# A sum on VectorE replaced by a casting and an adding transfer of GpSimd, in three pairs of row blocks

## The chip, the cores and the metric

The kernel runs on one core of a Trainium2 chip. The metric is the device time of one execution, in microseconds (us). Executions of the kernel before the change took 200.71 us (median of 3, 200.53 to 200.73). The engines are TensorE (PE; PEld is its weight load), VectorE (DVE), ScalarE (ACT), GpSimd (POOL) and SyncE (SP), which here only issues transfers.

## The reference, cut to what matters

The reference normalises x, and adds to x a linear attention of 32 heads and a gated feed-forward block:

```
xn = _layernorm(x, axis=-1)                       # x is 2048 x 512
return x + _A_ref(xn, A_wqkv, A_wo) + _B_ref(xn, B_w_gate, B_w_up, B_w_down)
# _B_ref: (silu(x @ w_gate) * (x @ w_up)) @ w_down, inner width 1792
# _A_ref: q, k, v = x @ wqkv; o = phi(q) (phi(k)^T v) / (phi(q) . sum phi(k)); o @ wo
```

The change lies in the last product, h @ w_down, where h = silu(x @ w_gate) * (x @ w_up) is 2048 x 1792.

## The kernel before, in words

The kernel lists every operation of every engine in one order written out by hand. A small recorder (`_Program`) gives each operation the semaphore waits that its reads and writes need, and each engine then takes its own operations strictly in that order. So an operation that waits holds up all that stands behind it on its engine. A transfer has a semaphore of its own, and whoever reads its result waits for that; the engine that issues it goes on.

Until about 154 us the kernel normalises and transposes x, makes q, k and the attention's matrix M, and makes h in transposed form (14 chunks of 128 columns). Rows 0 to 511 are finished on the way. The last stage, from about 154 us on, makes the output of rows 512 to 2047: six **pairs** p = 0 to 5 of row blocks, 128 rows each, `PAIRS = (10, 4, 12, 14, 6, 8)`, block `PAIRS[p]` and the next. A pair's h (256 rows x 1792) times w_down (1792 x 512) is a 2 x 2 block product, done with seven products in the place of eight (Strassen's way, in Winograd's form). It needs four sums of the quarters A11, A12, A21, A22 of h, each 128 x 896:

- `hcopy(p, i)` (L1055, ACT): scales one of four pieces of h into the pair's own buffers, in bf16. Piece 0 (7 chunks) holds A11 and A21, in buffer `Lo[p % 2]`; pieces 1, 2, 3 (2, 3 and 2 chunks) hold A12 and A22, in `Hi[p % 3]`. The tiles' names in the trace are those of the memory reused: `Lo` is wqkv or GT; `Hi` is xn, ef or xnT; piece 0 reads hT, piece 3 reads pq.
- `h_sum(p, i)` (L1067, DVE), in f16: S0 = A21 + A22, S1 = S0 - A11, S2 = A11 - A21, S3 = A12 - S1. The four lie in `Sd[p % 2]`.
- `dprod(p, i, ...)` (L1083, PE): product i, seven matmuls of 128x256. Products 5, 6, 7, 3 read S0, S1, S2, S3; products 1, 2, 4 read A11, A12, A22. `first(p)` is product 1 and the copy `dseed` (L1095, ACT); it is done in the pair before.
- `attn` (L1089, PE): four matmuls that add the attention of one block and one half of the columns; they read pk, which is q divided and transposed.
- `dkeep` (L1099, ACT), `dkeep_y` (L1103, DVE) and `du4` (L1109, DVE) carry partial results between banks of PSUM; `dout` (L1115, DVE) makes a 128 x 256 piece of output, and `store` (L692, SP) sends it.

Beside these runs the division of q for one block per pair, for use in later pairs: `den_sum` (L644, DVE), `den_turn` (L650, DVE, writes rden), `pq_mul` (L654, POOL, waits for rden), `turn` (L660, SP, a transposing transfer pk<-pq), and `pz_ahead` (L638, POOL, pz for the block two places on). There are two buffers of pz; the one made in pair p is read by the `den_sum` of pair p + 2, or by the second `den_sum` of pair 4.

In the order of pair p from 2 to 4, DVE takes S3 of p, den_sum, den_turn, dkeep_y, du4, one output, S0 of p + 1, one output, S1 of p + 1, one output, S2 of p + 1, one output. PE takes products 5 and 2 of p, two groups of attn, product 6, product 1 of p + 1, products 7 and 3, attn, product 4, attn. Which copies stand where on ACT is a table `HC`: key (pair, place), where place 0 is after dkeep, place 1 after dkeep_y, place 2 after `first(p + 1)`.

Nothing is issued as a transfer from GpSimd in the kernel before.

Of the kernel before, what the change touches and what calls it, by code (L numbers as in the profile page):

```python
# [7 lines left out]
ALU = mybir.AluOpType  # L8
# [109 lines left out]
def bass_parallel_sum__linear_attn_block__swiglu_ffn__prompt_kernel(nc, A_x, A_wqkv, A_wo, B_x, B_w_gate, B_w_up, B_w_down, out):  # L118
    xin = A_x[0]
    oview = out[0]  # L120
    K = _Program()
    bf, f32 = dt.bfloat16, dt.float32

    with contextlib.ExitStack() as es:
# [91 lines left out]
        def B(i):  # L216
            return ("bank", i)
# [424 lines left out]
        def den_sum(t):  # L642
            i = SLOT[t] % 2
            K.add("dve", lambda e: e.tensor_reduce(  # L644
                out=den[:, i, :], in_=pzh[i], axis=mybir.AxisListType.X, op=ALU.add),
                r=[("pz", i)], w=[("den", i)])

        def den_turn(t):
            i = SLOT[t] % 2
            K.add("dve", lambda e: e.reciprocal(rden[:, i, :], den[:, i, :]), r=[("den", i)], w=[("rden", i)])  # L650

        def pq_mul(t, after=()):
            i = SLOT[t] % 2
            K.add("pool", lambda e: e.tensor_tensor(  # L654
                out=heads(pq[:, t, :]), in0=heads(pq[:, t, :]),
                in1=rden[:, i, :][:, :, None].broadcast_to([P, NH, DH]), op=ALU.mult),
                r=[("pq", t), ("rden", i)] + list(after), w=[("pq", t)])

        def turn(t):
            K.add("sp", lambda e: e.dma_start_transpose(  # L660
                out=pk[:, SLOT[t], :].rearrange("p (g s) -> p g s", g=NG), in_=pq[:, t, :]),
                r=[("pq", t)], w=[("pk", SLOT[t])], dma=True)
# [323 lines left out]
        def split(ap):  # L986
            return ap.rearrange("p (s c) -> p s c", s=2)
# [13 lines left out]
        def wt(n):  # L1001
            return [("Wt", n, 0), ("Wt", n, 1)]

        def k7(ap):
            return ap.rearrange("p (k c) -> p k c", k=7)
# [9 lines left out]
        def t_sum(i, h):  # L1015
            own = {2: wtk, 3: [("xs", 0), ("xs", 1)], 4: late}[i]
            a, b, rk = {2: (Wt[2], Tt[1], [("Wt", 22, h)] + tk(1, h)), 3: (Tt[2], Wt[1], tk(2, h) + [("Wt", 11, h)]),
                        4: (Wt[3], Tt[2], [("Wt", 21, h)] + tk(2, h))}[i]
            K.add("dve", lambda e: e.tensor_tensor(
                out=Tt[i][:, h, :], in0=a[:, h, :], in1=b[:, h, :], op=ALU.subtract), r=rk, w=[("Tt", i, h)], a=own)  # L1020

        def tk(i, h=None):
            ks = [("Tt", i, g) for g in ((0, 1) if h is None else (h,))]
            return [k_ + (c,) for k_ in ks for c in (0, 1)] if i == 1 else ks
# [10 lines left out]
        def Av(p, i):  # L1035
            return (Lo[p % 2] if i % 2 == 0 else Hi[p % 3])[:, :, (i // 2) * P:(i // 2 + 1) * P]

        def Ak(p, j):
            return ("Lo", p % 2) if j == 0 else ("Hi", p % 3, j)
        Sd = [[xnf[:, 10 * D + 2 * N7:10 * D + 3 * N7], xnT[:, 0, 0:N7], pqf[:, 10 * D:10 * D + N7], xnT[:, 0, N7:2 * N7]],  # L1040
              [xnT[:, 1 + i // 2, (i % 2) * N7:(i % 2 + 1) * N7] for i in range(4)]]
        Sd = [[k7(s_.bitcast(f16)) for s_ in r] for r in Sd]
# [16 lines left out]
        H0, H1 = (0,), (1, 2, 3)  # L1059

        def h_sum(p, i):
            r = p % 2
            A11, A12, A21, A22 = [Av(p, j) for j in range(4)]
            S_ = Sd[r]
            a, b, op, hs, more = ((A21, A22, ALU.add, H0 + H1, []), (S_[0], A11, ALU.subtract, H0, [0]),
                                  (A11, A21, ALU.subtract, H0, []), (A12, S_[1], ALU.subtract, H1, [1]))[i]
            K.add("dve", lambda e: e.tensor_tensor(out=S_[i], in0=a, in1=b, op=op),  # L1067
                  r=[Ak(p, j) for j in hs] + [("Sd", r, j) for j in more], w=[("Sd", r, i)], a=sdk[r][i] if p < 2 else ())

        def dk(b):  # L1070
            return banks[b][:, 0:HD]

        def dprod(p, i, b, start, ks=range(7)):
            r = p % 2
            n = {5: 1, 6: 2, 7: 3, 4: 4, 1: 11, 2: 21, 3: 22}[i]
            cut, rk = (Tt[n], tk(n)) if n < 10 else (Wt[BS[n]], wt(n))
            if i in (1, 2, 4):
                L = Av(p, {1: 0, 2: 1, 4: 3}[i])
                lk = [Ak(p, j) for j in (H0 if i == 1 else H1) if any(0 <= k + 7 * (i > 1) - PIECE[j][0] < PIECE[j][1] for k in ks)]
            else:  # L1080
                j = {5: 0, 6: 1, 7: 2, 3: 3}[i]
                L, lk = Sd[r][j], [("Sd", r, j)]
            K.add("pe", [(lambda e, k=k: e.matmul(  # L1083
                split(banks[b][:, 0:HD]), L[:, k, :], cut[:, :, k * P:(k + 1) * P], start=(start and k == 0), stop=False,
                skip_group_check=True)) for k in ks], r=lk + rk, w=[B(b)])

        def attn(p, s_, lo, b):
            t = PAIRS[p] + s_
            K.add("pe", [(lambda e, g=g: e.matmul(dk(b), pk[:, SLOT[t], g * P:(g + 1) * P], M[:, g, lo:lo + HD], start=False,  # L1089
                                                  stop=(g == NG - 1), skip_group_check=True)) for g in range(NG)],  # L1090
                  r=[("pk", SLOT[t])] + [("M", g) for g in range(NG)], w=[B(b)])
# [5 lines left out]
        def dkeep(p):  # L1097
            r, d = p % 2, GB[p % 2][2]
            K.add("act", lambda e: e.activation(p5[:, r, 0:HD], dk(d), ACT.Copy), r=[B(d)], w=[("p5", r)])  # L1099
# [20 lines left out]
        def pz_ahead(t, after=()):  # L1120
            i = SLOT[t] + 2
            if i < NT:
                pz_mul(ORDER[i], after)
# [8 lines left out]
        for fc in range(NFC):  # L1132
# [13 lines left out]
            p = fc // 2  # L1146
# [65 lines left out]
        def first(p):  # L1212
            a, b, d = GB[p % 2]
            dprod(p, 1, a, True)
            dseed(p)

        DIV2 = {1: 15, 2: 6, 3: 7, 4: 9, 5: 8}
        HC = {(0, 1): [(1, 1), (1, 2), (1, 3)], (0, 2): [(2, 1), (2, 2), (2, 3)], (1, 0): [(2, 0)], (1, 1): [(3, 1)]}
        HC.update({(p, 2): [(p + 2, 0), (p + 2, 2)] for p in (1, 2, 3)})
        HC.update({(p, 0): [(p + 1, 3)] for p in (2, 3, 4)})  # L1220
        HC.update({(p, 1): [(p + 2, 1)] for p in (2, 3)})

        def copies(p, i):
            for v in HC.get((p, i), ()):
                hcopy(*v)
# [5 lines left out]
        for p in range(NP2 - 1):  # L1231
            a, b, d = GB[p % 2]
            t = DIV2.get(p)
            if p == 0:
                attn(p, 0, 0, a)
            dprod(p, 5, d, True)
            dkeep(p)
            if p == 0:
                t_sum(3, 0)
                t_sum(3, 1)  # L1240
                h_sum(0, 2)
            else:
                copies(p, 0)
                if p > 1:
                    h_sum(p, 3)
                den_sum(t)
                den_turn(t)
                pq_mul(t)
                turn(t)
            dprod(p, 2, a, False)  # L1250
            if p:
                attn(p, 0, 0, a)
            attn(p, 1, HD, d)
            dkeep_y(p)
            copies(p, 1)
            dprod(p, 6, b, False)
            if p == 0:
                first(1)
            du4(p, d)
            if p:  # L1260
                dout(p, 0, 0, a)
            if p == NP2 - 2:
                den_sum(DIV2[p + 1])
            if p == 0:
                h_sum(0, 3)
                t_sum(4, 0)
                t_sum(4, 1)
                copies(p, 2)
            else:
                if p == 1:  # L1270
                    h_sum(1, 3)
                h_sum(p + 1, 0)
                first(p + 1)
                copies(p, 2)
            dprod(p, 7, b, False)
            dout(p, 1, HD, b)
            if p == 0:
                dout(0, 0, 0, a)
                h_sum(1, 0)
            h_sum(p + 1, 1)  # L1280
            if p == NP2 - 2:
                den_turn(DIV2[p + 1])
            elif p:
                pz_ahead(t, [("Sd", 0, 0)] if p == 1 else [])
            dprod(p, 3, d, False)
            attn(p, 0, HD, d)
            dout(p, 0, HD, d)
            h_sum(p + 1, 2)
            if p == NP2 - 2:
                pq_mul(DIV2[p + 1], [("Sd", (p + 1) % 2, 2)])  # L1290
                turn(DIV2[p + 1])
            dprod(p, 4, b, False)
            attn(p, 1, 0, b)
            dout(p, 1, 0, b)
        p = NP2 - 1
# [58 lines left out]
```

## Time and profile before

| | |
|---|---|
| median of 3 runs | 200.71 us |
| the profiled execution | 200.89 us, its span 199.6 us |
| PE busy in the span | 195.1 us (98%) |
| DVE, ACT, POOL busy | 170.5, 153.6, 122.3 us |
| from the start of pair 2 to the end of pair 4 (169.69 to 190.97 us) | PE busy 7.09 of 7.09, 7.10 of 7.10, 7.09 of 7.09 us |
| the same, DVE busy | 6.78, 6.19, 6.22 us |
| the same, POOL busy | 2.17, 2.18, 1.06 us |

The profile is of one execution. Times in it count from the start of its span. The 1.3 us between span and time lie outside what it shows. A row of the timeline is: start, length, engine, line, operation, tile written <- tiles read, shapes, and in brackets how long the engine had been idle and what ended that.

### The profile page before, as it was taken

To read this page: it belongs to the slowest core of one execution; us is meant where nothing else is said; L and a number is where in the kernel's file an instruction comes from. 1 tells how busy PE (TensorE), PEld (TensorE's weight loads), DVE (VectorE), ACT (ScalarE), POOL (GpSimd) and SP (SyncE) were. 2 spreads that over 40 slices of the span, in tenths; PEclk is the share of its full clock that TensorE was granted. 3 is DMA by queue.
4 is the path that set the end of the run, shared out by engine and by line. 5 is a ranking of instruction groups with operands and counts; after the bars stand their busy time and mean duration, and the time that the engine had idled before them with its cause. 6 is when DMAs were issued, how large, how long until landed. Compare 5 with 4: busy or idle time off the path is not lost.

```text
span 199.6 us, 3566 instructions
## 1 busy us (share of the span) xinstructions
PE 195.1 (98%) x1193; PEld 114.8 (58%) x1207; DVE 170.5 (85%) x339; ACT 153.6 (77%) x308; POOL 122.3 (61%) x150
## 2 busy tenths in 40 slices
PE   8899999999999999999999999999999999999995
PEld 2344444444544445555555555555555888888884
DVE  2999998894797798988888998887799999998866
ACT  3799887749889988689898988888989968475200
POOL 3687876799995544787677666768877004413220
DMA  6943243289990000011111221000210012132223
GB/s 180 355 122 81 57 87 73 50 282 364 375 295 3 0 3 0 0 28 31 26 26 26 53 56 23 4 0 7 45 34 0 3 39 66 30 79 66 45 69 118
DMA packets 28899, 15.97 MB, mean 80 GB/s; under 512 B 17232, under 2 KB 28880, under 8 KB 28880
## 3 DMA queue, kind: packets, MB, share of 16 engines
q1 hardware_dynamic: 28320, 15.28, 27.3%
q10 hardware_dynamic: 560, 0.46, 0.7%
q8 instruction: 9, 0.15, 0.3%
q14 instruction: 10, 0.08, 0.1%
HBM read 9.70 MB, written 2.10 MB: 59 GB/s over the span
## 4 chain that ended last, share of the span: by engine, by line
PE 94%; DVE 2%; DMA 2%; issue 1%; ACT 0%; POOL 0%; SPq 0%
PE pb L846 32%; PE pb L1083 16%; PE pb L431 13%; PE pb L556 12%; PE pb L480 7%; PE pb L682 6%; PE pb L1089 5%; PE pb L686 2%; DMA x_sb<-in_A_x_dram 2%; PE pb L605 1%; PE pb L674 0%; DVE pq L470 0%; PE pb L398 0%; POOL ef L459 0%; DVE stats L298 0%
## 5 line engine op out<-in xcount | busy, mean ns | idle before, releaser
L654 POOL TENSOR_TENSOR pq<-pq,rden 128x512 bf16<-128x512 bf16 x16 | 16.9, 1056 | 36.7 <-DVE rden L650 23.1
L868 ACT ACTIVATE zacc<-pb,iw 128x384 bf16<-128x384 f32 x56 | 31.3, 590 | 5.9 <-PE pb L846 4.7
L431 PE MATMUL pb<-wqkv,xnT 128*128 128x512 bf16 x110 | 25.1, 379 | 0.2
L846 PE MATMUL pb<-xnT,wg 128*128 128x384 bf16 x112 | 25.1, 326 | 0.0
L638 POOL TENSOR_TENSOR pz<-pq,zbc 128x512 f32<-128x512 bf16 x16 | 18.6, 1164 | 5.3 <-DVE ef L808 3.8
L883 POOL TENSOR_TENSOR hT<-c,zacc 128x384 bf16<-128x384 f32 x18 | 16.1, 915 | 6.0 <-DVE c L879 4.0
L459 POOL TENSOR_SCALAR ef<-ef 128x512 bf16<-128x512 bf16 x25 | 15.5, 620 | 5.8 <-ACT ef L452 5.6
L879 DVE TENSOR_TENSOR c<-pb,p 128x384 f32<-128x384 f32 x28 | 15.5, 555 | 4.1 <-PE pb L846 2.8
L431 PEld LDWEIGHTS pb<-wqkv,xnT 128*128 128x128 bf16 x112 | 10.9, 98 | 13.3 <-DVE pk L470 0.4
L452 ACT ACTIVATE ef<-pb 128x512 bf16<-128x512 f32 x25 | 14.8, 593 | 3.9 <-PE pb L431 3.9
L874 DVE TENSOR_TENSOR pb<-pb,p 128x384 f32<-128x384 f32 x28 | 15.3, 561 | 1.7 <-PE pb L846 0.9
L497 POOL TENSOR_TENSOR zacc<-zacc,pk 128x512 f32<-128x512 f32 x13 | 15.4, 1181 | 1.0
L856 ACT ACTIVATE pb<-pb 128x384 f32<-128x384 f32 x28 | 12.7, 473 | 3.8 <-PE pb L846 2.9
L846 PEld LDWEIGHTS pb<-xnT,wg 128*128 128x128 bf16 x112 | 10.6, 98 | 7.7 <-ACT pb L856 0.8
L556 PE MATMUL pb<-xnT,wg 128*128 128x512 bf16 x56 | 14.7, 379 | 0.0
L556 PE MATMUL pb<-xnT,wu 128*128 128x512 bf16 x53 | 14.3, 379 | 0.1
L846 PE MATMUL pb<-xnT,wqkv 128*128 128x384 bf16 x56 | 13.7, 326 | 0.0
L846 PE MATMUL pb<-GT,wqkv 128*128 128x384 f16 x56 | 13.7, 326 | 0.0
L846 PE MATMUL pb<-wo,wqkv 128*128 128x384 f16 x56 | 13.7, 326 | 0.0
L298 DVE BATCH_NORM_STATS2 stats<-x_sb 128x6 f32<-128x512 bf16 x16 | 10.8, 678 | 3.0 <-DMA x_sb<-in_A_x_dram 3.0
L1089 PE MATMUL pb<-M,pk 128*128 128x256 bf16 x96 | 13.4, 273 | 0.0
L480 PE MATMUL pb<-pk,xn 128*128 128x512 bf16 x55 | 12.5, 379 | 0.1
(210 smaller groups left out, 488.6 us busy)
## 6 DMA issues: line engine op xcount, KB each, us to landing
x_sb<-in_A_x_dram SPq DMA_DIRECT2D x14, 128.0 KB, 4.5
wg<-in_B_w_gate_dram SPq DMA_DIRECT2D x2, 896.0 KB, 8.3
wu<-in_B_w_up_dram SPq DMA_DIRECT2D x2, 896.0 KB, 9.6
wd<-in_B_w_down_dram SPq DMA_DIRECT2D x2, 896.0 KB, 13.7
out_dram<-out_sb SPq DMA_DIRECT2D x24, 64.0 KB, 1.6
wqkv<-in_A_wqkv_dram SPq DMA_DIRECT2D x3, 256.0 KB, 5.0
wqkv<-in_A_wqkv_dram SPq DMA_DIRECT2D x1, 512.0 KB, 9.0
wo<-in_A_wo_dram SPq DMA_DIRECT2D x1, 512.0 KB, 10.0
```

Of the source, the lines that this page charges most:

```text
L431: K.add("pe", [(lambda e, c=c: e.matmul(banks[b][:, :], src[:, c, t * P:(t + 1) * P], wqkv[:, c, col:col + D], start=(c == 0), stop=(c == ...
L459: K.add("pool", lambda e: e.tensor_scalar(out=buf, in0=buf, scalar1=top, scalar2=0.0, op0=ALU.min, op1=ALU.max), r=[bkey] + tkeys, w=[bkey])
L480: K.add("pe", [(lambda e, c=c: e.matmul(banks[c][:, :], src[:, t, c * P:(c + 1) * P], pk[:, t, :], start=first, stop=last)) for c in range ...
L556: fns.append(lambda e, c=c, b=b, w_=w_: e.matmul(banks[b][:, :], w_[:, c, fc * P:(fc + 1) * P], xnT[:, c, C * 512:(C + 1) * 512], start=(c ...
L638: K.add("pool", lambda e: e.tensor_tensor(out=pzh[i][:, :, 0:DH], in0=heads(pq[:, t, :]), in1=heads(zbc[:, :]), op=ALU.mult), r=[("pq", t) ...
L654: K.add("pool", lambda e: e.tensor_tensor(out=heads(pq[:, t, :]), in0=heads(pq[:, t, :]), in1=rden[:, i, :][:, :, None].broadcast_to([P, N ...
L846: K.add("pe", [(lambda e, c=c: e.matmul(banks[bank][:, 0:TS], L[i][:, c, :], R[i][:, c, ts], start=(start and c == 0), stop=(c == 1), skip ...
L868: K.add("act", lambda e: e.activation(sil4[:, n, :], bk(bank), ACT.Silu, scale=iw[:, 0:1]), r=[B(bank), ("iw",)], w=[("sil4", n), ("zacc", ...
L879: K.add("dve", lambda e: e.tensor_tensor(out=c22[:, q, :], in0=bk(b), in1=p5[:, q, :], op=ALU.add), r=[B(b), ("p5", q)], w=[("c22", q)])
L883: K.add("pool", lambda e: e.tensor_tensor(out=hj(fc)[:, TB + q * TS:TB + (q + 1) * TS], in0=c22[:, q, :], in1=sil4[:, 2 * q + 1, :], op=AL ...
L1083: K.add("pe", [(lambda e, k=k: e.matmul(split(banks[b][:, 0:HD]), L[:, k, :], cut[:, :, k * P:(k + 1) * P], start=(start and k == 0), stop ...
L1089: K.add("pe", [(lambda e, g=g: e.matmul(dk(b), pk[:, SLOT[t], g * P:(g + 1) * P], M[:, g, lo:lo + HD], start=False, stop=(g == NG - 1), sk ...
```

## The change

The sums S0 of pairs 3, 4 and 5 are no longer made by DVE. In each of the pairs p = 2, 3, 4 GpSimd issues two transfers from one part of the core's memory to another: `h_acc(p + 1, 0)` copies A21 into S0's place, casting from bf16 to f16, and `h_acc(p + 1, 1)` adds A22 to it. The first stands ahead of pq_mul on POOL, the second behind it and ahead of pz_ahead. The second waits for the first to have landed. Both are 128 x 7 x 128 elements; the source lies in rows of 128 elements (256 bytes) with gaps, the destination is without gaps. S0 of pairs 0, 1 and 2 stays on DVE.

To have A22 complete sooner, piece 3 of pair p + 2 is copied by ACT at place 1 of pair p, behind piece 1, and no longer at place 0 of pair p + 1. This holds for pairs 3, 4 and 5.

```diff
+        def h_acc(p, i):
+            S_, src = Sd[p % 2][0], Av(p, 2 + i)
+            how = {} if i == 0 else dict(accum_op=ALU.add)
+            K.add("pool", lambda e: e.dma_start(S_, src, **how),
+                  r=[Ak(p, j) for j in (H1 if i else H0)] + ([("Sd", p % 2, 0)] if i else []), w=[("Sd", p % 2, 0)], dma=True)
...
-        HC.update({(p, 0): [(p + 1, 3)] for p in (2, 3, 4)})
-        HC.update({(p, 1): [(p + 2, 1)] for p in (2, 3)})
+        HC.update({(p, 1): HC.get((p, 1), []) + [(p + 2, 3)] for p in (1,)})
+        HC.update({(p, 1): [(p + 2, 1), (p + 2, 3)] for p in (2, 3)})
...
                 copies(p, 0)
                 if p > 1:
+                    h_acc(p + 1, 0)
+                if p > 1:
                     h_sum(p, 3)
                 den_sum(t)
                 den_turn(t)
                 pq_mul(t)
                 turn(t)
+                if p > 1:
+                    h_acc(p + 1, 1)
...
                 if p == 1:
                     h_sum(1, 3)
-                h_sum(p + 1, 0)
+                if p == 1:
+                    h_sum(2, 0)
                 first(p + 1)
                 copies(p, 2)
```

## The prediction

> **What bounds the kernel.** I read the chain that ended last first, then busy time by stretch for pairs 2 to 4, then the timeline of each engine there, then the transfers.
>
> ```profile
> PE 94%; DVE 2%; DMA 2%; issue 1%; ACT 0%; POOL 0%; SPq 0%
> ```
> ```profile
> 169.69:176.78 7.09, 7.09 (x67) 6.29 (x65) 6.78 (x14) 4.49 (x6) 2.17 (x2) 1.00 0.22 58
> 176.78:183.88 7.10, 7.10 (x68) 6.34 (x66) 6.19 (x13) 4.49 (x6) 2.18 (x2) 1.00 0.22 55
> 183.88:190.97 7.09, 7.09 (x67) 6.34 (x65) 6.22 (x15) 1.36 (x3) 1.06 (x1) 1.00 0.24 59
> ```
>
> The columns of the second fence are the stretch, its length, and busy PE, PEld, DVE, ACT, POOL, then clock, DMA share, GB/s. The stretches run from product 5 of a pair to product 5 of the next. PE has no gap: 65 matmuls at 0.109 us (0.765 us for seven, 172.09 to 172.85) are 7.09 us. The clock is full. DVE has 0.3 to 0.9 us spare in each. So work taken off DVE here shortens nothing; what can happen is that PE begins to wait.
>
> ```profile
> 169.69 0.93 PE L1083 MATMUL pb<-mixb,xn 128*128 128x256 f16 x7
> ...
> 176.78 0.93 PE L1083 MATMUL pb<-mixb,xnT 128*128 128x256 f16 x7
> ...
> 172.00 0.35 DVE L650 RECIPROCAL rden<-den 128x32 f32<-128x32 f32 x1
> ...
> 173.79 1.30 DVE L1067 TENSOR_TENSOR xnT<-GT,xn 128x896 f16<-128x896 bf16 x1
> 175.01 0.47 DVE L1115 SCALAR_TENSOR_TENSOR out_sb<-pb,iso,c 128x256 bf16<-128x256 f32 x1
> 175.40 0.61 DVE L1067 TENSOR_TENSOR xnT<-xnT,GT 128x896 f16<-128x896 f16 x1
> ...
> 178.66 0.35 DVE L650 RECIPROCAL rden<-den 128x32 f32<-128x32 f32 x1
> ...
> 167.83 1.17 POOL L638 TENSOR_TENSOR pz<-pq,zbc 128x512 f32<-128x512 bf16 x1 [1.56 <-DVE xn L1067]
> 172.43 1.05 POOL L654 TENSOR_TENSOR pq<-pq,rden 128x512 bf16<-128x512 bf16 x1 [3.43 <-DVE rden L650]
> 173.44 1.16 POOL L638 TENSOR_TENSOR pz<-pq,zbc 128x512 f32<-128x512 bf16 x1
> ```
>
> These are product 5 of pairs 2 and 3; DVE's rden of pair 2, S0 of pair 3 (the 1.30 row, slowed beside POOL; elsewhere 0.61), an output, S1 of pair 3, rden of pair 3; and POOL. See where the adding transfer must fit: behind pq_mul of pair 2 (ends 173.48), ahead of S1 (175.40) and product 5 (176.78).
>
> ```profile
> DMA packets 6470, 2.57 MB, mean 51 GB/s; under 512 B 3136, under 2 KB 6464, under 8 KB 6464
> ...
> q1 hardware_dynamic: 6464, 2.49, 18.8%
> ...
> out_dram<-out_sb SPq DMA_DIRECT2D x24, 64.0 KB, 1.6
> ...
> pk<-pq SPq DMA_TRANSPOSE x5, 2.4
> ```
>
> These are the transfers from 150 us on. A packet takes 0.188 x 49.6 x 16 / 6464 = 23 ns of one of 16 engines. The five transposing transfers are all there is under 512 bytes: 627 packets each, 2.4 us from issue to landing, of which SP issues for 1.2 us. A store of 128 packets lands in 1.6 us.
>
> **The change, part by part.**
>
> *S0 off DVE.* Three instructions (1.30, 0.87 and 0.61 us; 0.4 to 0.6 us of queue each) go. Worth 0: PE has no gap to close.
>
> *Piece 3 sooner on ACT.* In pair 1 one copy (0.71 us) comes ahead of dseed of pair 2. ACT was idle 0.50 us there, so dseed (166.63) and the two copies behind it move by 0.2 us; ACT's next idle time, 1.14 us before 170.65, takes that up, and dseed's bank is read by product 6 only at 172.09. In pairs 2 and 3 two short copies stand behind dkeep as before, only other ones. Cost 0, covered by those idle times. The buffers overwritten were last read by product 4 of a pair earlier (168.49 for the copy into ef, which now comes after 171).
>
> *The copying transfer.* POOL issues it after pz_mul (169.0) and piece 0 (168.9 with the shift). The adding one comes at 173.48, so it has 4.5 us to land at no cost. POOL itself is idle until 172.43; 3.4 us of issuing are free. If POOL issued longer, pq_mul would wait, and behind it turn on SP, whose pk is read two pairs on (180.18 plus 2.4 against attn of pair 4 at 185.41): cover enough.
>
> *The adding transfer* stands ahead of pz_mul on POOL. That pz is read by den_sum two pairs on (185.01) or in pair 4 (187.98), so up to 3 us of issue cost nothing. What waits for it is DVE (S1), then PE (product 5, which reads S0).
>
> Call its time from issue to landing X. No transfer is issued by GpSimd in this trace, so X is bounded. From below: the store, 1.6 us. Nearest row: the transposing transfer, inside the core's memory and in pieces of 256 bytes; this one has 128 x 7 = 896 pieces. Scaled: issue 1.2 x 896 / 627 = 1.7, pieces 896 x 23 ns / 16 = 1.3, and the rest of the 2.4 (2.4 - 1.2 - 0.9 = 0.3): 3.3 us for the copying one. The adding one reads its destination too; that is 0 to 1.3 us more, I take half: X = 4.0. From above: issue and pieces twice as dear, 2 x 3.0 + 0.3 = 6.3. I take 4.0, nearest to the row with the most alike pieces.
>
> Now the loop. S1 waits for the landing T. Behind it on DVE stand an output, S2, an output, S3, den_sum and rden: spacings 0.53 + 0.40 + 0.53 + 0.40 + 0.54 + 0.74 + 0.35 = 3.49 us (175.40 on, waits taken out). Then pq_mul, 0.08 + 1.05, and only then POOL issues the next pair's adding transfer. So T(next) = T + 3.49 + 1.13 + X, while PE needs T every 7.09 us.
> - Pair 3: T = 173.5 + 4.0 = 177.5; product 5 was at 176.78: PE waits 0.72.
> - Pair 4: T = 177.5 + 4.62 + 4.0 = 186.1; PE would be at 183.88 + 0.72: 1.5 more.
> - Pair 5: T = 194.7 against 190.97 + 2.2: 1.5 more.
> - In pair 5 the division of the last block hangs behind S1 and S2 as well: S2 ends T + 1.7, pq_mul T + 2.85, turn lands 2.4 later, T + 5.3; the attn that reads it stands at T + 5.03 (196.00 - 190.97). 0.3 more.
> - du4 of the pair comes T + 4.4, product 3 at T + 4.69: no wait.
>
> Sum 0 + 0 + 0.7 + 1.5 + 1.5 + 0.3 = 4.0 to 4.1 us, in general 3X - 8.2 + 0.3 once X is over 2.7. On the profiled execution 200.89 + 4.1 = 205.0; it is 0.2 above the median of the runs, so against that 200.7 + 4.1 = 204.8 us.
>
> The Trainium skill (DMA: Bandwidth & Descriptors, Anatomy of one DMA — SWDGE (gpsimd) path) gives a GpSimd transfer about 2.0 us and its bytes at 436 GB/s; by it 229 KB would take an estimated 2.5 us and the sum would be 0. No run here shows it yet.
>
> **Rivals.**
> - *The transfer is hidden* (X up to 2.7). For: the transposing one lands in 2.4, a store in 1.6. Against: 896 pieces, and an addition. Then T is 176.2, 183.5, 190.8, each ahead of PE; 200.7 us. The page just named says this.
> - *Much dearer transfers* (X over 5.3, POOL's issue slow, or small pieces moved twice). Then the copying one too overruns its 4.5 us. At X = 6.3 for both: the adding one is issued at 175.3, T = 181.6, 192.5, 203.4: 12.4 + 0.3 more, 213.4 us. For: nothing shows how GpSimd issues. Against: packets here cost 23 ns, and DMA is 22% busy. The Trainium skill (DMA: Bandwidth & Descriptors, Specifications) says that pieces under 512 bytes are read, modified and written, which speaks for this case; the transposing row already has such pieces.
> - *Faster*: DVE, freed of 0.6 us a pair, releases PE earlier. It would need PE waits on DVE. Among the waits from 160 us on there is one, 0.19 us before product 3 of pair 1 (167.27), ahead of all that moves. It decides only if DVE were the later one in pairs 2 to 5; at most 0.2 us, 200.5.
>
> **How the numbers follow.** About 0.2% (0.4 us) is what a measurement of this kernel can tell from no change. X from 2.7 to 5.3, chance 0.52: 200.9 to 208.7 us, likeliest 204.8. Hidden: 0.22. Over 5.3: 0.21. Faster: 0.05, hardly over 0.2%, so I leave 0.04 there and 0.01 to same. The range takes hidden and likeliest: 200.5 to 208.7, leaving out the dearest. Slower 0.73, same 0.23, faster 0.04.
>
> **What would show it.** Right: PE idle before product 5 of pairs 3, 4 and 5, put down to a DMA, growing 0.7, 1.5, 1.5; DVE idle before S1 in each; stretches of pairs 3 and 4 about 8.6 us long; POOL idle or issuing between pq_mul and pz_mul. Wrong: stretches still 7.09 (X small, or S1 not late), a wait of POOL's adding transfer on the copying one, pq_mul late because POOL still issues, or a longer start of the span.

## The result, and the profile after

The changed kernel takes 209.28 us (median of 4 runs, 208.74 to 209.97) against 200.72 us: 1.043 times, 95% interval 1.040 to 1.046. It is 8.6 us slower, where 4.1 us were forecast. The profiled execution took 209.47 us, its span 208.2 us, 8.6 us longer than before. In that profile product 5 of pair 2 starts 0.24 us later than before (169.93); a time to be compared across the two has to be shifted by that.

The chain that ended last, of the changed kernel:

```profile
PE 77%; issue 7%; POOL 6%; DMA 6%; DVE 2%; SPq 0%; POOLq 0%; DVEq 0%
```

Of that chain 94% was PE before. The stretches from product 5 to product 5, with the columns as in the prediction (length, then busy PE, PEld, DVE, ACT, POOL, clock, DMA share, GB/s); the last one runs from product 5 of pair 5 to the end:

```profile
169.93:179.17 9.24, 7.25 (x67) 6.23 (x65) 4.37 (x11) 4.48 (x6) 5.26 (x5) 1.00 0.77 102
179.17:189.29 10.12, 7.45 (x65) 6.18 (x66) 5.07 (x12) 4.48 (x6) 4.73 (x4) 1.00 0.67 87
189.29:199.22 9.93, 7.45 (x66) 6.19 (x66) 5.69 (x13) 0.75 (x2) 2.64 (x2) 1.00 0.59 80
199.22:208.00 8.78, 6.76 (x58) 5.38 (x58) 6.67 (x14) 0.38 (x1) 1.04 (x1) 1.00 0.32 91
```

Against 7.09, 7.10 and 7.09 before that is 2.15, 3.02 and 2.84 us more. With the 0.24 us of the later start and 0.3 us at the last attn it makes 8.55. Who waited for whom, from 160 us on (engine, tile, line, for whom; us in all, times, longest):

```profile
DVE xnT L1067 <- DMA xn<-ef: 4.3, 1, 4.3
DVE xnT L1067 <- DMA xnT<-xnT: 4.1, 1, 4.1
DVE xnT L1067 <- DMA xnT<-xn: 3.8, 1, 3.8
...
PE pb L1089 <- DMA xn<-ef: 2.4, 1, 2.4
PE pb L1089 <- DMA xnT<-xnT: 2.2, 1, 2.2
PE pb L1089 <- DMA xnT<-xn: 2.0, 1, 2.0
...
PE pb L1089 <- DVE pb L1115: 0.5, 2, 0.3
```

In each of the three pairs both S1 on DVE and product 5 on PE wait for the adding transfer (xnT<-xn in pair 3, xn<-ef in pair 4, xnT<-xnT in pair 5). Line numbers behind the new function have grown by six: L1089 is now dprod, L1095 attn, L1101 dseed, L1105 dkeep, L1115 du4, L1121 dout.

The loop stands in the timeline. One turn of it, from the landing in pair 3 to the landing in pair 4, in the rows of DVE and POOL:

```profile
173.68 1.68 POOL L1073 DMA_DIRECT2D xnT<-xn  x1
...
179.15 0.63 DVE L1067 TENSOR_TENSOR xnT<-xnT,GT 128x896 f16<-128x896 f16 x1 [3.84 <-DMA xnT<-xn]
...
182.29 0.35 DVE L650 RECIPROCAL rden<-den 128x32 f32<-128x32 f32 x1
...
182.74 1.05 POOL L654 TENSOR_TENSOR pq<-pq,rden 128x512 bf16<-128x512 bf16 x1 [5.30 <-DVE rden L650]
183.74 1.64 POOL L1073 DMA_DIRECT2D xn<-ef  x1
...
189.27 0.63 DVE L1067 TENSOR_TENSOR xnT<-xn,wqkv 128x896 f16<-128x896 f16 x1 [4.26 <-DMA xn<-ef]
```

Landing at 179.15, rden done at 182.64 (3.49 later), pq_mul done at 183.79, landing at 189.27: 10.12 us a turn, of which 5.5 are the transfer. What the six transfers took from issue to landing (KB, us), in order of time; the first and third lines are the copying ones of pairs 3 and 4, and the copying one of pair 5, with the name of the first, took 4.5 us:

```profile
xnT<-GT POOLq DMA_DIRECT2D x1, 224.0 KB, 3.6
...
xnT<-xn POOLq DMA_DIRECT2D x1, 224.0 KB, 5.4
xn<-wqkv POOLq DMA_DIRECT2D x1, 224.0 KB, 4.0
...
xn<-ef POOLq DMA_DIRECT2D x1, 224.0 KB, 5.5
...
xnT<-xnT POOLq DMA_DIRECT2D x1, 224.0 KB, 5.3
```

So X was 5.3 to 5.5 us, not 4.0. Put into the prediction's own sum, 3 x 5.4 - 8.2 + 0.3 = 8.3 us. The open questions were whether that sum holds (a loop, and nothing else), whether the moved copies or the relief of DVE count for anything, and what makes X so long.

### The profile page after: what moved, and what is told of

Read it like the earlier page. It is cut to its first block, busy times and chain, and to the rows that moved or that the text cites. A ratio compares the mean times of both kernels' runs of the same rounds, so it can differ in the third digit from the quotient of the medians.

```text
span 208.2 us, 3587 instructions
## 1 busy us (share of the span) xinstructions
PE 197.0 (95%) x1207; PEld 114.2 (55%) x1207; DVE 168.1 (81%) x336; ACT 153.4 (74%) x308; POOL 130.2 (63%) x156
## 4 chain that ended last, share of the span: by engine, by line
PE 77%; issue 7%; POOL 6%; DMA 6%; DVE 2%; SPq 0%; POOLq 0%; DVEq 0%
PE pb L846 31%; PE pb L431 13%; PE pb L556 12%; PE pb L480 7%; PE pb L682 6%; PE pb L1089 4%; DMA xnT<-xnT 3%; PE pb L1095 2%; DMA x_sb<-in_A_x_dram 2%; POOL xnT L1073 2%; POOL pq L654 2%; POOL pz L638 2%; PE pb L686 2%; POOL xn L1073 1%; DMA pk<-pq 1%
## 5 line engine op out<-in xcount | busy, mean ns | idle before, releaser
L638 POOL TENSOR_TENSOR pz<-pq,zbc 128x512 f32<-128x512 bf16 x16 | 19.9, 1247 | 5.3 <-DVE ef L808 3.8
L1105 ACT ACTIVATE p<-pb 128x256 f32<-128x256 f32 x6 | 2.3, 382 | 16.3 <-PE pb L1089 16.3
L1095 PE MATMUL pb<-M,pk 128*128 128x256 bf16 x96 | 13.4, 273 | 0.1
```

The lines of the kernel that those rows point to most:

```text
L638: K.add("pool", lambda e: e.tensor_tensor(out=pzh[i][:, :, 0:DH], in0=heads(pq[:, t, :]), in1=heads(zbc[:, :]), op=ALU.mult), r=[("pq", t) ...
```

## The experiments

**Without the addition.** Edit of the changed kernel:

```diff
-            how = {} if i == 0 else dict(accum_op=ALU.add)
+            how = {}
```

> Both transfers copy, none adds, so S0 is A22 alone (A21 is left out of the sum). Theory (a loop from the landing through S1, the rest of DVE's queue, rden and pq_mul to the next adding transfer, which costs 3X - 7.9 us in all, X being the time of the second transfer from issue to landing): a copying transfer landed in 3.6 to 4.0 us, so X = 4.0 and 200.7 + 4.1 = 204.8 us, PE waiting about 0.9, 1.5 and 1.5 us ahead of product 5 of pairs 3, 4, 5. Rival (GpSimd's transfers disturb everything beside them, by their number and packets): number and packets are the same, so the time stays over 208 us.

Measured: 205.27 us (205.14 to 205.85), 1.022 times the kernel before (1.020 to 1.025), 4.6 us more. The second transfer landed in 4.1, 4.2 and 4.3 us, the first in 3.6, 3.4 and 3.2. The sum gives 3 x 4.2 - 7.9 = 4.7. PE's waits ahead of product 5:

```profile
177.97 0.94 PE L1089 MATMUL pb<-mixb,xnT 128*128 128x256 f16 x7 [0.70 <-DMA xnT<-xn]
...
186.75 0.94 PE L1089 MATMUL pb<-mixb,xn 128*128 128x256 f16 x7 [1.08 <-DMA xn<-ef]
...
195.62 0.94 PE L1089 MATMUL pb<-mixb,xnT 128*128 128x256 f16 x7 [1.16 <-DMA xnT<-xnT]
```

The number of transfers and of pieces is unchanged and 4 us are gone, so disturbance by their mere number is out. It also splits X. A plain copy in the second place takes 0.5 to 1.1 us longer than one in the first place. In the second place SP issues turn at the same moment, and turn itself then lands in 4.3 to 4.4 us, against 2.4 to 2.5 for those that pairs 2 to 4 issue in the kernel before. In this place the addition takes another 1.2 us.

**Only the copies moved.** Edit: both calls of h_acc go, S0 is back on DVE in every pair; the table HC stays changed.

```diff
-                if p > 1:
-                    h_acc(p + 1, 0)
...
-                if p > 1:
-                    h_acc(p + 1, 1)
...
-                if p == 1:
-                    h_sum(2, 0)
+                h_sum(p + 1, 0)
```

> S0 of all pairs is back on DVE, no transfer of GpSimd; only the copies of piece 3 stay a third of a pair sooner. Theory: ACT's idle time covers them, 200.7 us. Rival (the moved copies delay dseed or dkeep and are part of the loss): 201.2 to 203 us, with PE waiting on ACT in pairs 2 to 4.

Measured: 200.73 us, ratio 0.999 (0.998 to 1.001). The moved copies cost nothing that can be measured.

**No S0 at all in pairs 3 to 5.** Edit: the calls of h_acc go, and nothing takes their place (`h_sum(2, 0)` alone stays).

> S0 of pairs 3, 4 and 5 is made by nobody (products and sums read what an earlier pair left there), the rest as in the changed kernel. So DVE is relieved at no price. Theory: PE has no gap to close, 200.7 us, within 0.2. Rival (DVE's relief is worth something, and the transfers hide it): 200.1 us or less.

Measured: 200.73 us, ratio 1.000 (0.999 to 1.002). From 169 to 190 us DVE had 5.23 to 6.05 us to do in each 7 us, PE 7.00 of 7.00; one of the three stretches:

```profile
176.00:183.00 7.00, 7.00 (x67) 6.26 (x65) 5.23 (x12) 4.39 (x7) 2.18 (x2) 1.00 0.25 65
```

Work taken off DVE for nothing gains nothing. This is the ceiling of the idea: in this order of work no way to make S0 elsewhere can make the kernel faster.

**The transfers issued sooner.** Edit: the copies of piece 0 a third of a pair sooner, both transfers of pair p + 2 in pair p.

```diff
-        HC.update({(p, 2): [(p + 2, 0), (p + 2, 2)] for p in (1, 2, 3)})
...
+        HC.update({(p, 1): [(p + 2, 0), (p + 2, 1)] for p in (1, 2, 3)})
+        HC.update({(p, 2): [(p + 2, 2), (p + 2, 3)] for p in (1, 2, 3)})
...
             copies(p, 1)
+            if p in (1, 2, 3):
+                h_acc(p + 2, 0)
...
             attn(p, 0, HD, d)
+            if p in (1, 2, 3):
+                h_acc(p + 2, 1)
```

> The same six transfers, issued about half a pair to a pair sooner: ACT copies piece 0 of pair p + 2 (and piece 1) at place 1 of pair p, pieces 2 and 3 at place 2; the copying transfer of pair p + 2 stands behind pq_mul of pair p, the adding one behind pz_ahead of pair p. Theory (only the late issue and the length count): lands at about 176.8, 182.9 and 190.8 against PE's 176.8, 183.9 and 191.0, so 200.7 to 201.3 us, faster than the changed kernel by 8 us. Rival (disturbance by the transfers, or POOL's time for issuing): stays over 204 us.

Measured: 203.00 us (202.94 to 203.12), 1.011 times (1.009 to 1.012). Of the 8.6 us 6.3 are gone, but 2.3 stay, where I had expected at most 0.6. The rows of POOL show where the second transfer loses its time:

```profile
174.02 0.98 POOL L1073 DMA_DIRECT2D xn<-wqkv  x1
175.01 1.18 POOL L638 TENSOR_TENSOR pz<-pq,zbc 128x512 f32<-128x512 bf16 x1
179.32 1.66 POOL L1073 DMA_DIRECT2D xn<-ef  x1 [3.13 <-DMA xn<-wqkv]
```

At the new place the copying transfer takes 4.8 us for pair 4 and 5.6 for pair 5, against 3.5 for pair 3. Those two run beside turn (for pair 4 SP issues it at 174.09) and also beside the adding transfer of the pair before, still under way (for pair 4 issued at 171.21); this run does not tell the two apart. The adding one behind waits 3.1 and 3.4 us on POOL and itself takes 5.6, 5.7 and 5.2 (pairs 3, 4, 5). So it lands at 185.0 and 192.7 for pairs 4 and 5, where 182.9 and 190.8 were expected. I had carried over 4.0 us from another place.

**One pair alone.** Edit: h_acc in pair 5 alone, or in pair 3 alone, S0 on DVE in the other pairs.

```diff
-                if p > 1:
-                    h_acc(p + 1, 0)
+                if p == 4:                       # p == 2 for pair 3 alone
+                    h_acc(p + 1, 0)
...
-                if p == 1:
-                    h_sum(2, 0)
+                if p + 1 != 5:                   # 3
+                    h_sum(p + 1, 0)
```

> The two transfers in pair 5 alone, S0 of pairs 3 and 4 on DVE. Theory (loop): nothing is late before it, pq_mul of pair 4 ends at about 187.3, the transfer lands 5.4 later at 192.7 against 191.0, 0.3 more at the last attn: 2.0 us, 202.7 us. Rival (each pair pays its third of the 8.6 us by itself): 203.6 us.

> The two transfers in pair 3 alone, S0 of pairs 4 and 5 on DVE. Theory (loop): PE waits 2.1 us ahead of product 5 of pair 3 and 0.4 us ahead of product 7, which waits for du4; then nothing is late any more: 2.5 us, 203.2 us; together with the run of pair 5 alone 4.5 us, about half of 8.6. Rival (each pair pays by itself): 203.6 us, and the two runs together 5.7 us.

Measured: pair 5 alone 203.84 us (203.12 to 204.90), 1.016 times (1.011 to 1.020); pair 3 alone 203.42 us (203.29 to 203.65), 1.013 times (1.011 to 1.016). That is 3.2 and 2.8 us, 5.9 together: the rival's figure, not mine. The four runs of pair 5 alone lie 1.8 us apart, so its 3.2 is loose; the profiled one is the fastest, 2.5 us above the kernel before. In its trace the copying transfer took 4.6 us, for a reason that is not shown (turn is issued only 4.0 us after it), and the adding one waited 0.9 us for it, which I had not counted. In the trace of pair 3 alone PE loses 2.0 us from product 5 to product 5 and 0.4 us from there to product 7, about what I had named, and 0.3 us more ahead of product 4. The brackets count only idle time, which is a little less:

```profile
178.54 0.94 PE L1089 MATMUL pb<-mixb,xnT 128*128 128x256 f16 x7 [1.84 <-DMA xnT<-xn]
...
182.91 0.94 PE L1089 MATMUL pb<-xs,xnT 128*128 128x256 f16 x7 [0.27 <-DVE pb L1115]
...
185.21 0.94 PE L1089 MATMUL pb<-wg,xn 128*128 128x256 f16 x7 [0.16 <-DVE out_sb L1121]
```

By their times, these two runs fit a price that each pair pays by itself as well as a loop, or better. They could not tell the two apart, since a pair alone pays waits behind S1 (product 7, product 4) that the loop hides when the next landing is late anyway. The run after the next was made for that.

**What the length of a transfer is made of.** Edit: pair 3 reads rows without gaps, pair 4 casts nothing.

```diff
             S_, src = Sd[p % 2][0], Av(p, 2 + i)
+            if p == 3:
+                S_ = S_.rearrange("p k c -> p (k c)")
+                src = (Hi[p % 3] if i else Lo[p % 2]).rearrange("p k s -> p (k s)")[:, 0:7 * P]
+            if p == 4:
+                S_ = S_.bitcast(bf)
```

> Three pairs, three kinds of transfers, whose times to landing are read one by one. Pair 3: source rows of 1792 bytes without gaps (the wrong columns of the pieces, so the sum is of other data). Pair 4: pieces of 256 bytes as in the changed kernel, but no cast (the sum is made in bf16 and read as f16). Pair 5: unchanged. If the 896 pieces make the length: pair 3 lands in about 2 us (copying) and 2.5 us (adding), pairs 4 and 5 in 4.0 and 5.4 us. If the addition itself is dear by the byte: the adding one of pair 3 stays 1.4 us above the copying one. If the cast is: pair 4 is shorter than pair 5. By the loop with 2.5, 5.4 and 5.4 us the time is 206 us.

Measured, in one run: 207.35 us, where 206 were expected. From issue to landing, copying and adding: pair 3 (128 pieces of 1792 bytes) 2.5 and 3.8 us; pair 4 (no cast) 3.1 and 5.5; pair 5 (unchanged) 4.6 and 5.3. With 3.8, 5.5 and 5.3 the sum gives 6.7 us, 207.4; I had taken 2.5 for the first of the three. Pieces of 256 bytes cost the adding transfer 1.5 us more than long ones. For the copying one the same place has to be compared: in pair 3 it took 3.6 us in the changed kernel, so 1.1 more (the 4.6 of pair 5 ran beside the adding transfer of pair 4). The addition costs 1.3 us even on long pieces; the cast costs the adding transfer nothing. For the copying one it may matter, but places and times differ (3.1 in pair 4 against 4.0 there in the changed kernel), and one run does not settle that.

**The adding transfer ahead of pq_mul.** Edit: one call moved.

```diff
                 den_turn(t)
+                if p > 1:
+                    h_acc(p + 1, 1)
                 pq_mul(t)
                 turn(t)
-                if p > 1:
-                    h_acc(p + 1, 1)
```

> The changed kernel with one thing moved: on POOL the adding transfer stands ahead of pq_mul of its pair and not behind it, so it no longer waits for rden, which stands behind S1 on DVE; it waits for the copying transfer alone. Theory (the loop through rden and pq_mul is what makes pairs 4 and 5 dear): issued at about 172.9, 180.4 and 188.5, landing 5 us later, PE waits 1, 0.5 and 0.7 us and 0.4 us in pairs 3 and 4 for du4: 203 to 204.5 us. Rival (each pair pays its own price, no loop): only what the earlier issue saves, 0.6 to 0.8 us a pair, 207 to 207.5 us.

Measured: 203.88 us (203.68 to 204.09), 1.017 times (1.015 to 1.018). The adding transfer is hardly shorter: it took 5.3, 5.2 and 5.2 us. What is gone is the wait for rden. It was issued at 172.53, 180.55 and 188.22, and PE's waits ahead of product 5 do not grow from pair to pair but shrink, to none in pair 5:

```profile
177.84 0.94 PE L1089 MATMUL pb<-mixb,xnT 128*128 128x256 f16 x7 [1.32 <-DMA xnT<-xn]
...
185.83 0.94 PE L1089 MATMUL pb<-mixb,xn 128*128 128x256 f16 x7 [0.27 <-DMA xn<-ef]
...
193.49 0.94 PE L1089 MATMUL pb<-mixb,xnT 128*128 128x256 f16 x7
```

5.4 of the 8.6 us went with a place in a queue. Three separate prices would have left 207 us or more, as reckoned in the expectation. So the loop through rden and pq_mul is shown, by this run and by the turn of it in the timeline above.

**Long pieces in all three pairs, with the addition and without.** Edit, and the second with `how = {}` as well:

```diff
-            S_, src = Sd[p % 2][0], Av(p, 2 + i)
+            S_ = Sd[p % 2][0].rearrange("p k c -> p (k c)")
+            src = (Hi[p % 3] if i else Lo[p % 2]).rearrange("p k s -> p (k s)")[:, 0:7 * P]
```

> The changed kernel with the source of all six transfers read in rows of 1792 bytes without gaps (the first 896 elements of each row of the buffer, the wrong columns, so the sum is of other data), 128 pieces in the place of 896. The adding transfer landed in 3.8 us in the one pair where this was tried. Theory (3X - 7.9): 204.2 us. Rival (the number of transfers counts, not their length): over 207 us.

> As the run before, and the second transfer copies and does not add. By the runs so far the adding costs about 1.2 us, so X = 2.6, just under the 2.7 us from which the loop costs something. Theory: 200.7 to 201.2 us, PE without waits on a DMA. Rival (a transfer issued by GpSimd has a price of its own, whatever its length): 203 us or more.

Measured: 204.27 us (204.14 to 204.51), 1.018 times (1.017 to 1.020), with X = 3.9 in all three pairs; and 200.65 us, ratio 1.001 (1.000 to 1.002), with X = 2.6, 2.7 and 2.7. In the latter PE shows no gap from pair 2 to pair 5, though DVE still waits 1.0 to 1.4 us for each landing:

```profile
176.46 0.93 PE L1090 MATMUL pb<-mixb,xnT 128*128 128x256 f16 x7
183.55 0.93 PE L1090 MATMUL pb<-mixb,xn 128*128 128x256 f16 x7
190.65 0.93 PE L1090 MATMUL pb<-mixb,xnT 128*128 128x256 f16 x7
```

The four kernels with the same order of work give the line of the sum:

| second transfer | X, us | 3X - 7.9 | measured more than before, us |
|---|---|---|---|
| long pieces, no addition | 2.7 | 0.2 | 0.1 |
| long pieces, addition | 3.9 | 3.8 | 3.7 |
| 256-byte pieces, no addition | 4.2 | 4.7 | 4.6 |
| 256-byte pieces, addition (the change) | 5.4 | 8.3 | 8.6 |

## Why the prediction was wrong, step by step

- *PE bounds the stage, and DVE's relief is worth 0*: right, shown by the run without S0.
- *Piece 3 sooner on ACT costs 0*: right, shown by the run with the copies alone.
- *The copying transfer lands inside its 4.5 us*: right in the changed kernel (3.6, 4.0, 4.5), with less to spare than the 3.3 us of the sum. In pair 5 alone it took 4.6, and the adding one waited for it.
- *The loop, and 3X - 8.2 + 0.3*: right, over a range of X from 2.7 to 5.4, and by the run that opened the loop.
- *X = 4.0*: wrong; this is the step that failed. The adding transfers landed in 5.3 to 5.5 us, and since the sum counts X three times, 1.4 us became 4.2. Three sizes in it were off.
  - The addition. The prediction wrote "that is 0 to 1.3 us more, I take half". In this place it measured 1.2 us (5.3 to 5.5 with it, 4.1 to 4.3 without), near the far end of that bound.
  - The copying part, 3.3 us. It was scaled from a transposing transfer of "627 packets", but that number divides all 3136 small packets among the five transposing transfers, and some belong to the stores (48 of them from 176.4 to 180.1 us in the trace before, where only stores run). From 173.4 to 176.0 us, where one transposing transfer runs, there are 544 packets under 512 bytes. With 544 the same scaling gives 2.0 + 1.3 + 0.4 = 3.7 us, and the first copying transfer took 3.6.
  - The place. The sum priced a transfer by itself. A plain copy in the second place took 4.1 to 4.3 us, 0.5 to 1.1 more than in the first, and this was in no term. That turn makes the whole of it is not shown, though the two are issued within 0.1 us and turn is slower too. For the adding transfer the moment of turn matters less: issued 0.9 us behind turn (pair 5 alone) it took 5.0 us, and 2.8 us ahead of turn (the run that opened the loop) 5.2 to 5.3, against 5.3 to 5.5 beside it. "DMA is 22% busy" was the wrong witness: it is an average over a stretch without these transfers, and with them it was 59 to 77%.
- *The range*: the time lies 0.6 us above it, in the rival "X over 5.3", given 0.21; but that rival's own picture, a copying transfer that overruns its 4.5 us, did not come about.
- *du4 comes before product 3: no wait*: wrong in its place. The wait for du4 is at product 7, which writes the bank that du4 reads, 0.4 us by the starts in pairs 3 and 4. It cost nothing there, since DVE and POOL set the pace; it did cost in pair 3 alone.
- *The Trainium skill's price for a GpSimd transfer* (DMA: Bandwidth & Descriptors, Anatomy of one DMA — SWDGE (gpsimd) path; an estimate of 2.5 us for these bytes): the runs agree for long pieces without an addition (2.2 to 2.9 us) and not for 256-byte pieces (3.1 to 4.6, more in the run that issued them sooner), nor with an addition (3.9 and 5.4). Its statement that pieces under 512 bytes are read, modified and written (same page, Specifications) spoke for the dear case; small pieces did cost more, 1.5 us between long and short adding transfers, but no run shows that this is the reason.

## What to carry to other kernels

Before moving work off an engine, look whether the engine that sets the pace ever waits for it; in pairs 2 to 5 it never did, and nothing could be won. A transfer put between two engines' queues has to be priced in its place (beside what is issued at the same moment) and by its pieces. And ask what must happen before the next one can be issued: where the landing releases the work that releases the next issue, every microsecond too many is paid at each turn, and moving the issue ahead of that work can be worth as much as a faster transfer (here 5.4 us, against 5.0 for long pieces).

## What the runs showed of the hardware

- GpSimd's issue of a transfer of 128 x 1792 bytes read 0.58 us in 128 pieces and 0.97 us in 896, each about 0.2 us more for the first of a kernel; with the addition the rows read 0.9 and 1.65 us, and the next instruction of POOL, started meanwhile, was slower by 0.3 to 0.7 us (pz_ahead 1.47 and 1.85 for 1.17).
- Landing of a copying transfer: 2.2 to 2.9 us (128 pieces) and 3.1 to 4.6 us (896 pieces); up to 5.6 us in 896 pieces beside both a transposing and an adding transfer. With the addition: 3.8 to 3.9 us (128 pieces) and 5.0 to 5.7 us (896).
- The transposing transfer pk<-pq, at a median of 2.4 us before, is slower beside a transfer of GpSimd: 2.6 us in the changed kernel, 4.0 with long pieces, 3.2 with long pieces and no addition, 4.3 to 4.4 with 256-byte pieces and no addition.
